# Transposing loads for the last three blocks of h and its gradients, in place of a plain load and TensorE transposes

## The chip, the cores and the metric

The kernel runs on one core of one Trainium2 chip. The metric is device time in microseconds (us) of one execution. Three runs of the kernel before gave 505.66, 508.24 and 508.82 us; the median is 508.24 us.

## The reference: what is computed

x, k, v and the incoming gradient `go` have 2048 rows and 512 columns, in bf16. The forward part is a sum of three things: x itself, a gated long convolution, and a gated feed-forward block on the normalised rows xn.

```python
xn = layernorm(x)
g, u = xn @ w_gate, xn @ w_up          # 2048 x 1376
h = g * u
out = x + conv_part(xn, k, v, shift_k, ssm_k, ssm_D) + h @ w_down
```

The program returns `out` and the gradients of all nine inputs. For the change, three of these matter: the gradients of w_down (`out_9`, 1376 x 512, h transposed times go) and of w_gate and w_up (`out_7` and `out_8`, 512 x 1376, xn transposed times the gradients of g and u). All three contract over the 2048 rows.

## The kernel before, in words

**Stages.** The first 300 us compute, for eight chunks of 256 rows each, the feed-forward block and its backward part, beside the spectral transforms of the convolution. For each chunk, `ffn1` makes three products of 1376 columns by 256 rows: h and the two gradients. They are called slots t = 0 (h), 1 and 2 (the gradients). TensorE makes them with the 1376 columns on the partitions, in 11 blocks of 128 columns (the last has 96). The first seven chunks (`NCH - 1`) are stored to the DRAM scratch tensor `HDD[P, NFB, NCH - 1, 3, 256]`, which is indexed by partition, block, chunk, slot and row; the last chunk stays in SBUF in `hds[1]`.

**The last stage**, from about 320 us on, is where the change lies. The generator `dw` walks over the 11 blocks `fb`. The weight gradients contract over the rows, so each block needs h and its gradients turned, with the 128 rows of a tile on the partitions. For that, a block is loaded back from `HDD` with one plain load of 1344 KB (`load_hb`, L799), two or three blocks ahead, into one of two buffers of the tag `hb`. `hid_t(fb, t)` (L804 to L816) then turns one slot: 16 TensorE transposes of 128 x 128 into a PSUM tile `pt` (L815; 14 from `hb`, 2 from `hds[1]`), and one ScalarE copy of 128 x 2048 from PSUM into `nath` (slot 0) or `natd` (slots 1 and 2). That copy goes through the helper `act` at L221.

In each block, in program order: 16 matmuls `pd` (L922) give the w_down gradient of the block from `nath`; the copy `od` and its store (L925); `hid_t(fb + 1, 0)` and `hid_t(fb + 1, 1)`; 32 matmuls `pu` (L939) from `natd` for columns c = 0 and 1; `hid_t(fb + 1, 2)` and `load_hb(fb + 3)`; 32 more `pu` matmuls; the copy `og`; after every second block two stores (L952). `natd` has two buffers and `nath` has one.

**Beside it** run generators that `dw` advances step by step (L1063): `inv_y` and `inv_dk` (inverse transforms on TensorE: `po` at L892, loads `gk` at L877, stores of `o5t` at L895), `dsk_gram`, and `ew`, which is the VectorE tail: `final(b)` and `bwd(b)` for eight pairs of rows. `final` loads `bb` one step ahead (L1000) and stores `o` (L1013) and `e` (L1028), each from a single buffer; `bwd` stores `dk` (L994). Near the end, `put_dD` copies a column on VectorE (L903) and transposes it on TensorE (`ptd`, L906).

**Order.** In this stage every DMA is issued from SyncE's queue (SP), in order. A planner fixes the order on each engine ahead of the run: it simulates the engines by its own costs, and among the instructions that are ready it takes the one that the program names first. An instruction whose buffer isn't free yet is ordered behind the ones that free it.

**Transposing loads already there.** `load_xt` (L475) fetches xn and go of chunks 1 to 7 with `dma_start_transpose`, 128 rows by 1024 columns (256 KB) each, 12 in all, between 31 and 241 us.

Of the kernel before, what the change touches and what calls it, by code (L numbers as in the profile page):

```python
# [8 lines left out]
BF = mybir.dt.bfloat16  # L9
# [11 lines left out]
R = 16  # L21
P = 128
NC4 = 4
FBLK = [(i * 128, min(128, F - i * 128)) for i in range((F + 127) // 128)]
NFB = len(FBLK)
NCH = 8
# [150 lines left out]
def kernel(  # L177
# [24 lines left out]
    nc = tc.nc  # L202
# [14 lines left out]
    def cs(c):  # L217
        return slice(c * 128, (c + 1) * 128)

    def act(o, i):  # L220
        nc.scalar.copy(o, i)  # L221
# [10 lines left out]
    HDD = dram.tile([P, NFB, NCH - 1, 3, 256], BF, name="HDD")  # L232
# [5 lines left out]
    def P2(name, shape, dt=F32):  # L238
        return ps2.tile(shape, dt, name=name, tag="p2")

    def P1(name, shape, dt=F32):
        return ps1.tile(shape, dt, name=name, tag="p1")

    ident = const.tile([P, P], BF, name="ident")
# [27 lines left out]
    hds = [p.tile([P, NFB, 3, 256], BF, name=f"hd{i}") for i, p in enumerate((hdp, hdl))]  # L272
# [497 lines left out]
    for tag in mainit:  # L770
        if tag == "wa":
            wa_es.close()
            c1 = ctx.enter_context(tc.tile_pool(name="c1", bufs=1, reuse_waits="tile"))
            xnC = c1.tile([P, R, D], BF, name="xnC")
            goC = c1.tile([P, R, D], BF, name="goC")
# [11 lines left out]
    c1n = ctx.enter_context(tc.tile_pool(name="c1n", bufs=1, reuse_waits="tile"))  # L787
    c1b = ctx.enter_context(tc.tile_pool(name="c1b", bufs=2, reuse_waits="tile"))
    nats = {}
# [6 lines left out]
    def load_hb(fb):  # L796
        f0, fw = FBLK[fb]
        t = c1b.tile([P, NCH - 1, 3, 256], BF, name="hb")
        nc.sync.dma_start(t[:fw], HDD[:fw, fb])  # L799
        hbs[fb] = t  # L800

    hbs = {}

    def hid_t(fb, t):  # L804
        f0, fw = FBLK[fb]
        hb = hbs.pop(fb) if t == 2 else hbs[fb]
        if t == 0:
            nats[fb, 0] = c1n.tile([P, R, P], BF, name="nath")
        elif t == 1:
            nats[fb, 1] = c1n.tile([P, 2, R, P], BF, name="natd", bufs=2)  # L810
        dst = nats[fb, 0] if t == 0 else nats[fb, 1][:, t - 1]
        pt = P2("pt", [P, R, P], BF)
        for r in range(R):
            hs = hb[:fw, r // 2, t] if r < R - 2 else hds[1][:fw, fb, t]
            nc.tensor.transpose(pt[:, r, :fw], hs[:, (r % 2) * 128:(r % 2) * 128 + 128], ident[:fw, :fw])  # L815
        act(dst[:, :, :fw], pt[:, :, :fw])  # L816

    load_hb(0)
    pend = [load_g1(0, 0), load_g1(1, 0)]
# [91 lines left out]
    def dw():  # L911
        og = None
        for t in range(3):
            hid_t(0, t)
            yield
        load_hb(2)
        for fb, (f0, fw) in enumerate(FBLK):
            last = fb + 1 == NFB
            nt = nats.pop((fb, 0))
            pd = P1("pd", [P, D])  # L920
            for r in range(R):
                nc.tensor.matmul(pd[:fw, :], lhsT=nt[:, r, :fw], rhs=goC[:, r, :], start=(r == 0), stop=(r == R - 1))  # L922
            od = c2b.tile([P, D], BF, name="od")
            act(od[:fw], pd[:fw])
            nc.sync.dma_start(out_9[f0:f0 + fw, :], od[:fw])  # L925
            yield
            if not last:
                hid_t(fb + 1, 0)
                yield
                hid_t(fb + 1, 1)  # L930
                yield
            ng = nats.pop((fb, 1))
            pu = P2("pu", [P, NC4, 2, P])
            if fb % 2 == 0:
                og = c2.tile([P, 2, NC4, 2 * P], BF, name="og")
            q0 = (fb % 2) * P
            for c in range(NC4):
                for r in range(R):
                    nc.tensor.matmul(pu[:, c, :, :fw], lhsT=xnC[:, r, cs(c)], rhs=ng[:, :, r, :fw],  # L939
                                     start=(r == 0), stop=(r == R - 1))  # L940
                if c == 1:
                    yield
                    if not last:
                        hid_t(fb + 1, 2)
                        if fb + 3 < NFB:
                            load_hb(fb + 3)
                        yield
            act(og[:, :, :, q0:q0 + fw].rearrange("p t c f -> p c t f"), pu[:, :, :, :fw])
            if fb % 2 == 1 or last:
                a = f0 - q0  # L950
                for t, o in enumerate((out_7, out_8)):
                    nc.sync.dma_start(o[:, a:f0 + fw].rearrange("(c p) f -> p c f", p=128), og[:, t, :, :q0 + fw])  # L952
            yield
# [110 lines left out]
    for n, _ in enumerate(dw()):  # L1064
        for sd in sides:
            if n >= sd[0]:
                sd[0] += sd[1]
                next(sd[2], None)
# [33 lines left out]
```

## Time and profile before

| quantity | value |
|---|---|
| median of three runs | 508.24 us |
| the profiled execution: its time / its span | 507.66 us / 505.9 us |
| TensorE busy over the span | 479.2 us (95%) |
| VectorE, ScalarE busy | 341.0 us (67%), 328.7 us (65%) |
| mean DMA rate | 278 GB/s |
| L815 transposes on TensorE | 528, first at 324.8 us, last at 488.0 us |
| L799 plain loads of `hb` | 11, at 315.7 to 461.0 us, 6.9 to 11.9 us to landing |

The span runs from the first to the last instruction; the execution's own time is 1.76 us more. A matmul's row gives its duration through the pipeline (218 ns for a transpose), although the next one starts earlier: 16 transposes in a row take 0.9 us. A row of SP gives how long the issue of a DMA held SP, not how long the data took; the time to landing counts from the start of the issue.

### The profile page before, as it was taken

To read this page: it belongs to the slowest core of one execution; us is meant where nothing else is said; L and a number is where in the kernel's file an instruction comes from. 1 tells how busy PE (TensorE), PEld (TensorE's weight loads), DVE (VectorE), ACT (ScalarE), POOL (GpSimd) and SP (SyncE) were. 2 spreads that over 40 slices of the span, in tenths; PEclk is the share of its full clock that TensorE was granted. 3 is DMA by queue.
4 is the path that set the end of the run, shared out by engine and by line. 5 is a ranking of instruction groups with operands and counts; after the bars stand their busy time and mean duration, and the time that the engine had idled before them with its cause. 6 is when DMAs were issued, how large, how long until landed. Compare 5 with 4: busy or idle time off the path is not lost.

```text
span 505.9 us, 10724 instructions
## 1 busy us (share of the span) xinstructions
PE 479.2 (95%) x4420; PEld 323.4 (64%) x4457; DVE 341.0 (67%) x633; ACT 328.7 (65%) x358; POOL 6.7 (1%) x17
## 2 busy tenths in 40 slices
PE   8789889998999999999999999999999989999996
PEld 7677554645747547547457733566776768777885
DVE  3987998888365748866648956031288987999800
ACT  3676788857837949759569975286575524555551
POOL 3000000000000000000000000020000000000000
PEclk9998999999999999999999999999999999999999
DMA  9999997989896957967968396999999999897513
GB/s 279 375 330 335 292 298 250 341 269 344 299 296 212 278 187 242 289 206 233 271 198 264 127 343 222 374 359 370 375 334 342 371 294 351 269 309 240 166 60 108
DMA packets 98045, 140.41 MB, mean 278 GB/s; under 512 B 18474, under 2 KB 72047, under 8 KB 96108
## 3 DMA queue, kind: packets, MB, share of 16 engines
q1 hardware_dynamic: 96668, 138.94, 83.3%
q10 hardware_dynamic: 1328, 0.79, 0.5%
q8 instruction: 35, 0.57, 0.5%
q14 instruction: 14, 0.11, 0.1%
HBM read 72.76 MB, written 63.41 MB: 269 GB/s over the span
## 4 chain that ended last, share of the span: by engine, by line
PE 55%; DMA 20%; DVE 10%; ACT 9%; issue 3%; SPq 2%; ACTq 0%
PE px L534 12%; PE pgu L493 9%; PE pu L939 8%; PE py L527 6%; PE pdh L499 5%; PE pd L922 4%; DMA FD<-fst 3%; PE pg L590 2%; PE pt L815 2%; PE ps L561 2%; ACT gu L221 2%; DMA out_dram<-o 2%; DMA khC<-in_A_k_dram 2%; DMA bb<-BX 2%; ACT fst L221 2%
## 5 line engine op out<-in xcount | busy, mean ns | idle before, releaser
L939 PE MATMUL pu<-natd,xnC 128*128 128x256 bf16 (+1 forms) x704 | 79.1, 270 | 0.7 <-ACT nath L221 0.7
L534 PE MATMUL px<-WT,hd 128*128 128x512 bf16 (+1 forms) x346 | 78.9, 379 | 0.5 <-issue 0.3
L939 PEld LDWEIGHTS <-xnC 128*128 128x128 bf16 x704 | 67.2, 98 | 8.7 <-issue 1.0
L534 PEld LDWEIGHTS <-hd 128*128 128x128 bf16 (+1 forms) x352 | 33.5, 98 | 42.7 <-issue 3.7
L221 ACT COPY natd<-pt 128x2048 bf16<-128x2048 bf16 (+1 forms) x22 | 40.4, 1838 | 25.4 <-PE pt L815 25.4
L493 PE MATMUL pgu<-xt,Wu 128*128 128x256 bf16 (+1 forms) x352 | 53.3, 274 | 3.5 <-DVE WdT L224 2.0
L493 PE MATMUL pgu<-xt,Wg 128*128 128x256 bf16 (+1 forms) x352 | 52.8, 273 | 0.0
L221 ACT CAST gu<-pgu 128x1024 bf16<-128x1024 f32 (+1 forms) x48 | 45.3, 946 | 11.3 <-PE pgu L493 11.0
L221 ACT CAST GO<-pg 128x1024 bf16<-128x1024 f32 x48 | 46.3, 1019 | 7.7 <-issue 4.8
L577 DVE TENSOR_TENSOR T<-SP 128x2048 bf16<-128x2048 bf16 x24 | 29.3, 1223 | 31.9 <-ACT SP L221 31.9
L499 PE MATMUL pdh<-gt,WdT 128*128 128x256 bf16 (+1 forms) x352 | 47.1, 275 | 1.5 <-DVE WdT L224 1.3
L221 ACT CAST SP<-ps 128x1024 bf16<-128x1024 f32 x48 | 46.6, 1034 | 1.9 <-PE ps L561 1.9
L221 ACT CAST fst<-pf 128x1024 bf16<-128x1024 f32 x40 | 39.2, 1034 | 12.5 <-DMA FD<-fst 10.8
L493 PEld LDWEIGHTS <-Wu 128*128 128x128 bf16 (+1 forms) x352 | 33.0, 100 | 19.9 <-issue 15.1
L527 PE MATMUL py<-Wd,hd 128*128 128x512 bf16 (+1 forms) x166 | 40.5, 380 | 0.8 <-issue 0.5
L499 PEld LDWEIGHTS <-WdT 128*128 128x128 bf16 (+1 forms) x352 | 34.9, 101 | 6.8 <-DVE WdT L224 1.5
L922 PE MATMUL pd<-goC,nath 128*128 128x512 bf16 (+1 forms) x166 | 38.3, 379 | 0.5
L221 ACT CAST bx<-px 128x512 bf16<-128x512 f32 x16 | 9.5, 592 | 45.1 <-PE px L534 45.1
L493 PEld LDWEIGHTS <-Wg 128*128 128x128 bf16 (+1 forms) x352 | 34.9, 100 | 3.6
L511 DVE TENSOR_TENSOR hd<-gu 128x512 bf16<-128x512 bf16 (+1 forms) x48 | 19.1, 398 | 24.3 <-ACT gu L221 24.2
L512 DVE TENSOR_TENSOR hd<-gu,dh 128x1024 bf16<-128x1024 bf16 (+1 forms) x48 | 30.7, 642 | 1.1 <-ACT dh L221 0.2
L527 PEld LDWEIGHTS <-hd 128*128 128x128 bf16 (+1 forms) x176 | 16.3, 98 | 22.8 <-issue 4.8
(155 smaller groups left out, 677.7 us busy)
## 6 DMA issues: line engine op xcount, KB each, us to landing
HDD<-hd SPq DMA_DIRECT2D x35, 384.0 KB, 4.8
hb<-HDD SPq DMA_DIRECT2D x10, 1344.0 KB, 11.4
FD<-fst SPq DMA_DIRECT2D x24, 512.0 KB, 3.9
X<-FD SPq DMA_DIRECT2D x24, 512.0 KB, 5.5
GD<-GO SPq DMA_DIRECT2D x24, 512.0 KB, 3.8
g<-GD SPq DMA_DIRECT2D x8, 1024.0 KB, 8.8
BX<-bx SPq DMA_DIRECT2D x8, 512.0 KB, 3.4
bb<-BX SPq DMA_DIRECT2D x8, 512.0 KB, 7.6
```

The lines of the kernel that those rows point to most:

```text
L221: nc.scalar.copy(o, i)
L493: nc.tensor.matmul(pgu[:w, i, t, :], lhsT=W[:, c, f0:f0 + w], rhs=xt[:, :, c, :], start=(c == 0), stop=(c == NC4 - 1))
L499: nc.tensor.matmul(pdh[:w, i, :], lhsT=WdT[:, c, f0:f0 + w], rhs=gt[:, :, c, :], start=(c == 0), stop=(c == NC4 - 1))
L511: nc.vector.tensor_tensor(hd[:fw, fb0:fb0 + n, 0, :], gu[:fw, :n, 0, :], gu[:fw, :n, 1, :], op=ALU.mult)
L512: nc.vector.tensor_tensor(hd[:fw, fb0:fb0 + n, 1:3, :], gu[:fw, :n], dh[:fw, :n].unsqueeze(2).to_broadcast((fw, n, 2, 256)), op=ALU.mult)
L527: nc.tensor.matmul(py[:], lhsT=hd[:fw, fb, 0, ss], rhs=Wd[:fw, fb, :], start=(fb == 0), stop=(fb == NFB - 1))
L534: nc.tensor.matmul(px[:], lhsT=hd[:fw, fb, t, ss], rhs=W[:fw, fb, :], start=(t == 1 and fb == 0), stop=(t == 2 and fb == NFB - 1))
L561: nc.tensor.matmul(ps[32 * q:32 * q + 32, a, :], lhsT=TB.EF[64 * a:64 * a + 64, 4 * g + q, ri].rearrange("p k j -> p (k j)"), rhs=X[64 * a ...
L577: tt(W[:].rearrange("p c a d -> p c (a d)"), A[:, i:i + 1].rearrange("p c a d -> p c (a d)").to_broadcast((P, 2, 2 * D)), B[:].rearrange(" ...
L590: nc.tensor.matmul(pg[q // 2][64 * a:64 * a + 64, q % 2, :], lhsT=TB.EI[32 * q:32 * q + 32, 2 * g + a, yi].rearrange("p k c -> p (k c)"), ...
L922: nc.tensor.matmul(pd[:fw, :], lhsT=nt[:, r, :fw], rhs=goC[:, r, :], start=(r == 0), stop=(r == R - 1))
L939: nc.tensor.matmul(pu[:, c, :, :fw], lhsT=xnC[:, r, cs(c)], rhs=ng[:, :, r, :fw], start=(r == 0), stop=(r == R - 1))
```

## The change

The last three blocks (8, 9, 10) no longer have a plain load or 48 TensorE transposes each. `load_nat` fetches h (d = 0) and the two gradients (d = 1) of such a block from `HDD` by transposing loads on SP, one for each of the seven stored chunks: 128 partitions by 256 columns for h, by 512 columns for the gradients. The eighth chunk is turned as before from SBUF, by six transposes in one PSUM tile (`last_t`), with two smaller copies. For h, the new tile takes a buffer of the tag `hb`; the gradients take the two buffers of `natd`.

The loads of h of block fb + 3 stand where its `load_hb` stood, in the middle of block fb; those of the gradients of block fb + 2 stand at the end of block fb. The tiles are laid out by chunk in all 11 blocks, so the copies of `hid_t` and the operands of `pd` and `pu` are indexed differently throughout.

```diff
+    def load_nat(fb, d):
+        if d:
+            nats[fb, 1] = t = c1n.tile([P, NCH, 2, 2, P], BF, name="natd", bufs=2)
+        else:
+            nats[fb, 0] = t = c1b.tile([P, NCH, 1, 2, P], BF, name="nathT", tag="hb")
+        for ch in range(NCH - 1):
+            nc.sync.dma_start_transpose(out=t[:, ch].rearrange("s t h f -> s (t h) f"),
+                                        in_=HDD[:, fb, ch, d:1 + 2 * d].rearrange("p t s -> p (t s)"))
+
+    def last_t(fb):
+        f0, fw = FBLK[fb]
+        pt = P2("pt7", [P, 3, 2, P], BF)
+        for t in range(3):
+            for h in range(2):
+                nc.tensor.transpose(pt[:, t, h, :fw], hds[1][:fw, fb, t, h * 128:h * 128 + 128], ident[:fw, :fw])
+        act(nats[fb, 0][:, NCH - 1, 0, :, :fw], pt[:, 0, :, :fw])
+        act(nats[fb, 1][:, NCH - 1, :, :, :fw], pt[:, 1:3, :, :fw])
+
+    TURNED = range(NFB - 3, NFB)
+
     def hid_t(fb, t):
+        if fb in TURNED:
+            if t == 0:
+                last_t(fb)
+            return
...
-            nats[fb, 0] = c1n.tile([P, R, P], BF, name="nath")
+            nats[fb, 0] = c1n.tile([P, NCH, 1, 2, P], BF, name="nath")
         elif t == 1:
-            nats[fb, 1] = c1n.tile([P, 2, R, P], BF, name="natd", bufs=2)
+            nats[fb, 1] = c1n.tile([P, NCH, 2, 2, P], BF, name="natd", bufs=2)
...
-        act(dst[:, :, :fw], pt[:, :, :fw])
+        act(dst[:, :, :, :fw], pt[:].rearrange("s (c h) f -> s c h f", h=2)[:, :, :, :fw])
...
-                nc.tensor.matmul(pd[:fw, :], lhsT=nt[:, r, :fw], rhs=goC[:, r, :], start=(r == 0), stop=(r == R - 1))
+                nc.tensor.matmul(pd[:fw, :], lhsT=nt[:, r // 2, 0, r % 2, :fw], rhs=goC[:, r, :], start=(r == 0), stop=(r == R - 1))
...
-                    nc.tensor.matmul(pu[:, c, :, :fw], lhsT=xnC[:, r, cs(c)], rhs=ng[:, :, r, :fw],
+                    nc.tensor.matmul(pu[:, c, :, :fw], lhsT=xnC[:, r, cs(c)], rhs=ng[:, r // 2, :, r % 2, :fw],
...
                         hid_t(fb + 1, 2)
-                        if fb + 3 < NFB:
+                        if fb + 3 in TURNED:
+                            load_nat(fb + 3, 0)
+                        elif fb + 3 < NFB:
                             load_hb(fb + 3)
...
+            if fb + 2 in TURNED:
+                load_nat(fb + 2, 1)
             act(og[:, :, :, q0:q0 + fw].rearrange("p t c f -> p c t f"), pu[:, :, :, :fw])
```

More of the change, by code (lines that the diff above doesn't have):

```diff
@@ L807, in hid_t @@
         if t == 0:
-            nats[fb, 0] = c1n.tile([P, R, P], BF, name="nath")
+            nats[fb, 0] = c1n.tile([P, NCH, 1, 2, P], BF, name="nath")
         elif t == 1:
-            nats[fb, 1] = c1n.tile([P, 2, R, P], BF, name="natd", bufs=2)
-        dst = nats[fb, 0] if t == 0 else nats[fb, 1][:, t - 1]
+            nats[fb, 1] = c1n.tile([P, NCH, 2, 2, P], BF, name="natd", bufs=2)
+        dst = nats[fb, 0][:, :, 0] if t == 0 else nats[fb, 1][:, :, t - 1]
         pt = P2("pt", [P, R, P], BF)
```

## The prediction

> **What bounds the kernel now.** I read the slices of the page first: TensorE is at nine tenths or more almost everywhere, so the question is where it is last in line. The change touches only the stage from 428 us on, so I went to the chain that ended last, in order of time (start, us, what):
>
> ```profile
> 467.25 0.91 PE pt L815 x16
> 468.16 0.02 issue
> 468.18 0.02 ACTq L221
> 468.20 0.04 issue
> 468.24 1.87 ACT nath L221
> 470.11 0.04 issue
> 470.15 3.65 PE pu L939 x32
> 473.81 0.89 PE pt L815 x16
> 474.70 3.49 PE pu L939 x32
> ...
> 496.17 5.29 PE pu L939 x64
> ```
>
> From 409 us to 501.5 us the chain never leaves TensorE, except for the copy at 468.24 and its two like. During that copy TensorE turns the next slot and does a `po`; its own idle time there is 0.22 us. So here the transposes stand on the path that sets the end, and each us of them that goes is a us gained, as long as what replaces them is in time.
>
> What replaces them is issued by SP. The rows of L475 (duration min/median/max in ns is how long SP was held):
>
> ```profile
> L475 SPq DMA_TRANSPOSE xt<-XN x5: 1276/1292/3196, 71.3 to 237.4; - x5
> L475 SPq DMA_TRANSPOSE gt<-in_grad_out_dram x5: 1322/1588/3988, 72.6 to 240.9; - x5
> L475 SPq DMA_TRANSPOSE gt<-go_b x1: 1364/1364/1364, 31.2 to 31.2; - x1
> L475 SPq DMA_TRANSPOSE xt<-xn_b x1: 3220/3220/3220, 48.2 to 48.2; - x1
> DMA to landing us min/median/max: 3.8/4.6/8.2
> ```
>
> No transposing load here held SP for less than 1.28 us. SP's timeline shows what a plain issue costs, and the places that the new loads take:
>
> ```profile
> 445.61 0.34 SPq L1028 DMA_DIRECT2D out_dram<-e  x1
> 446.92 0.28 SPq L979 DMA_DIRECT2D out_dram<-dskt  x1
> 447.30 0.34 SPq L799 DMA_DIRECT2D hb<-HDD  x1
> ...
> 458.62 0.59 SPq L877 DMA_DIRECT2D gk<-GD  x1
> ...
> 461.01 0.38 SPq L799 DMA_DIRECT2D hb<-HDD  x1
> ```
>
> A plain load of 1344 KB holds SP for 0.34 to 0.38 us, and there is room between the issues.
>
> **The change, part by part.**
>
> *TensorE, removed.* A full slot is 16 transposes in 0.89 us, 56 ns each; in block 10 (96 columns) 0.68 us, 42 ns each. Each block goes from 48 to 6, so 42 go: 42 x 56 ns = 2.35 us in blocks 8 and 9, 42 x 42 ns = 1.8 us in block 10; together 6.5 us. The two waits of 0.22 us on the copy ahead of `pu`, those of 454.87 and 470.15, go as well: 0.4 us. **Gain on the path: 6.9 us.** If all else is in time, `pu` of block 10 ends at 501.5 - 6.9 = 494.6 us.
>
> *ScalarE.* Nine copies (six of 1.86 us, three of 1.44 us) go; six small ones come. By 0.58 us for 512 elements and 1.01 us for 1024 (`od`, `og`) these are some 0.4 and 0.6 us. ScalarE was idle about half the time here, so this counts as nothing beyond the 0.4 us.
>
> *Layout in all blocks.* The 24 remaining copies now write pieces. The row nearest to that is `o5t`, which writes with a stride and takes 1.02 us for 1024 elements beside 0.99 us of `og`; I take nothing, at most 0.03 us per 1024 elements, hidden by ScalarE's idle time. `pu` reads two runs of 128 elements per matmul both before and after, only closer together; no row prices the distance, and I take nothing.
>
> *DMA data.* Three plain loads (1344 + 1344 + 1008 KB) go, 21 x 64 KB + 21 x 128 KB = 4032 KB come. The bytes hardly change. In the windows of 10 us the DMA engines' share here is 0.96, 0.64, 1.00, 0.44, 0.25 from 440 to 490 us, so there is room behind 470 us.
>
> *SP, added.* Three issues of 0.38 us become 42 transposing ones: 7 + 7 per block. No row has a transposing load of 64 or 128 KB. From below, it can't hold SP for less than a plain issue, 0.28 us; from above, the longest one measured held it 3.99 us, and the mean of the 12 is 1.94 us. How does the hold go with size? Plain issues hardly depend on it: 0.33 us for `od` of 128 KB, 0.46 us for `khC` of 2048 KB. And the quiet transposing issues lie close together, 1.28 to 1.36 us, like a fixed cost. So I stay by the nearest row, 1.28 us for the same kind of instruction, and take off little for the smaller size: **1.25 us**, an estimate.
>
> By the Trainium skill, Advanced Engine Details and Errata, section DMA Advanced Topics, transposing DMAs on this chip are as fast as regular ones. For landing this trace agrees (4.6 us median beside 3.3 to 6.9 us for plain loads of 256 KB), for the hold on SP it doesn't (1.28 us beside 0.3 to 0.6 us); if it held for both, the second rival below would be the outcome. The same skill, VectorE: DVE Perf Modes, section The three transpose paths, gives 1309 ns for one 128 x 128 by DMA and 390 ns by TensorE and prefers TensorE; paid for each tile one after the other, 3 x 42 tiles would be 165 us by that page. The trace speaks against that: eight such tiles landed 3.8 us after the issue began.
>
> *What SP must get through.* `nathT` of block 8 is issued from 428.3 us, where its `hb` load was, and costs nothing: SP has time until 444 us. From 444.1 us, when the last transposes of block 7 free the `hb` buffer, there are always loads waiting: h of 9 at once, gradients of 8 when `pu` of block 6 ends (447.7 us), gradients of 9 about 460 us, h of 10 about 464 us (it takes the buffer of h of block 8, so it waits for `pd` of block 8), gradients of 10 about 472 us. That is 35 transposing issues. Between them, 18 other DMAs that the timeline shows between 445.6 and 482.6 us (`e`, `dk`, `o`, `od`, `o5t`, `og`, one `gk`, `dskt`); counted without the time in which a full queue held them they are 7.2 us. Between issues lies about 0.08 us, 53 times: 4.2 us. With a hold of 1.25 us: 43.8 + 7.2 + 4.2 = 55.2 us, so the last issue ends at 499.3 us and began at 498.0. It lands 3.8 us later (the shortest landing, since it is smaller): 501.8 us. `pu` of block 10 needs that piece in its first of four groups; behind it are 50 of 64 matmuls, 50/64 x 5.29 = 4.1 us. End of `pu`: 506.0 us, beside 501.5 us before: **+4.5 us**. The gain on TensorE is spent waiting in front of `pu` of block 9 (its loads end about 486 us, it would like to start at 477 us) and of block 10.
>
> In general the shift is 34 us for each us of hold: nothing changes at 1.12 us, and the full 6.9 us is gained at 0.92 us and below.
>
> *Others behind SP.* A run of seven issues holds SP for about 9 us. The stores of `o` and `e` wait behind it, and VectorE writes these single buffers again about 12 us later, landing of 4 to 6 us included. So VectorE's tail (its end was at 479.3 us) slips by some us at each run. The column for `ptd` is its last work, and TensorE reached `ptd` at 482.9 us; so some of the wait may show there instead. `gk` has 20 us between its issue and its use, enough.
>
> **Rivals.**
>
> 1. *SP is the bound with a hold of 1.12 to 1.4 us* (my forecast): 507.66 + 4.5 = 512.2 us, between 507.7 and 517.2 us. For it: the quiet rows at 1.28 us. Against: nothing so small was measured.
> 2. *The hold falls with size, to 0.92 us or less; SP keeps up*: 507.66 - 6.9 = 500.8 us. For it: 1.28 us was paid for eight tiles, here there are two or four. Against: plain issues don't fall with size.
> 3. *The hold is that of a busy queue*, slower. Place: the same 35 issues. Three of the 12 held SP for 3.2 us or more, where 512 KB transfers stood ahead of them in full DMA engines. The other nine average 1.43 us, all 12 average 1.94 us: 507.66 + 34 x (1.43 - 1.12) = 518.2 us up to 507.66 + 34 x 0.82 = 535.5 us. It decides once the mean hold is over 1.4 us. For it: the new loads read pieces of 512 and 1024 bytes where L475 reads 2 KB, and stores of `o`, `e`, `dk` and `og` mix in. Against: with SP the bottleneck the DMA engines have less to do (64 KB per 1.25 us is 52 GB/s).
> 4. *It doesn't do what it says*: the planner, which has its own costs, puts the loads so late or SP's stores so early that block 8 already starves. Then time like rival 3.
>
> **How the numbers follow.** Forecast 1 has a chance of 0.50, rival 2 has 0.25, rival 3 has 0.20, rival 4 has 0.05. The predicted time is that of forecast 1, 512 us; it is made against the profiled execution (507.66 us), which is 0.6 us below the median of the runs. The range of 500 to 522 us takes in rivals 1 and 2 and the lower end of 3. Within 1% of 508.24 us (503.2 to 513.3 us, about what a measurement can tell from no change) lies a good half of forecast 1 and little of rival 2: 0.34. Slower by more: the rest of forecast 1, rivals 3 and 4: 0.40. Faster by more: 0.26.
>
> **What would show it.** In the profile after: 384 transposes at L815 and 18 of `last_t`, 24 big copies in place of 33; TensorE busy less by 6 to 7 us. The rows of the transposing issues decide: a median hold of 1.2 to 1.3 us with SP issuing without a pause from 444 to about 498 us, and TensorE waiting for `natd` ahead of the last `pu` groups, bears out forecast 1. Holds under 0.9 us and no wait of `pu` on a DMA mean rival 2. I am wrong altogether if TensorE waits somewhere that hangs on neither SP nor these loads.

## The result, and the profile after

The changed kernel takes 524.53 us (median of 5 runs, 522.09 to 525.51) where the kernel before takes 507.75 us (median of 5 runs on the same chip, 505.53 to 508.82). The ratio is 1.0336, with a 95% interval of 1.0309 to 1.0364: 3.4% slower. The forecast was 512 us with a range of 500 to 522 us; the result lies above the range. The profiled execution took 523.57 us, with a span of 521.5 us.

The page of the kernel after: the busy time of each engine, the TensorE clock in 40 slices (tenths of full speed, 13 us each), and the chain that ended last, by engine.

```profile
PE 481.4 (92%) x4331; PEld 318.5 (61%) x4331; DVE 341.2 (65%) x633; ACT 315.7 (61%) x355; POOL 6.8 (1%) x17
...
PEclk9999999999999999999999999999999999997698
...
PE 55%; DMA 14%; DVE 10%; SPq 10%; ACT 8%; issue 3%; ACTq 0%; DVEq 0%
```

ScalarE lost the copies that were taken out (328.7 to 315.7 us). TensorE has fewer instructions and yet more busy time (479.2 to 481.4 us), because its clock drops in the last slices. And SP's queue, 2% of the chain before and absent from it behind 409 us, now makes 10%. Here is the end of that chain of the kernel after, in order of time (start, us, what):

```profile
452.51 1.02 SPq L811
453.54 0.05 issue
453.59 1.24 SPq L811
...
508.53 2.90 DMA natd<-HDD
511.43 0.04 issue
511.47 5.67 PE pu L964 x52
```

From 452 us the chain goes from one transposing issue of L811 to the next, up to the last one; between 468.5 and 477.4 us it passes through a store of `dk`, VectorE and a few plain issues. In SP's own timeline no gap from 452.25 us to the end of the last issue at 509.8 us is over 0.12 us. The last data land at 511.43 us, and the last matmuls of the kernel follow. That SP would set the end was the forecast. The rows of these issues (min/median/max in ns of the time that SP was held; the last line is that of `natd`):

```profile
L811 SPq DMA_TRANSPOSE nathT<-HDD x21: 1182/1244/1957, 427.6 to 497.8; - x21
L811 SPq DMA_TRANSPOSE natd<-HDD x21: 1211/1264/2845, 461.4 to 508.5; - x21
...
DMA to landing us min/median/max: 2.4/2.8/6.6
```

The medians, 1.244 and 1.264 us, are the 1.25 us of the estimate. So the hold was right, and something else is 11 us off. SP's timeline of the kernel after shows where it begins:

```profile
427.64 8.40 SPq L811 DMA_TRANSPOSE nathT<-HDD  x6
436.14 0.52 SPq L1057 DMA_DIRECT2D out_dram<-e  x1
...
450.55 0.35 SPq L1042 DMA_DIRECT2D out_dram<-o  x1
451.15 0.33 SPq L1057 DMA_DIRECT2D out_dram<-e  x1
451.86 0.29 SPq L1008 DMA_DIRECT2D out_dram<-dskt  x1
452.25 9.02 SPq L811 DMA_TRANSPOSE nathT<-HDD  x7
```

The store of `e` at 436.14 us stands behind six transposing issues that began at 427.64 us. And the second run of issues begins at 452.25 us, where the prediction had 444.1 us: it stands behind stores of `o`, `e` and `dskt`, whose data VectorE had not made. Why VectorE was late is in two lines of its timeline (in brackets its idle time before the instruction, and what ended it):

```profile
440.54 0.69 DVE L1044 TENSOR_TENSOR e<-goC,yC 128x1024 bf16<-128x1024 bf16 x1 [6.39 <-DMA out_dram<-e]
...
471.24 0.69 DVE L1019 TENSOR_TENSOR dk<-dks,skb 128x1024 bf16<-128x1024 bf16 x1 [7.66 <-DMA out_dram<-dk]
```

VectorE may not write `e` again until the store of the old `e` has landed. That store had been held by SP's transposing issues. So SP and VectorE hold each other: SP's run delays a store, the store delays VectorE, VectorE delays the next stores, and SP, in order, delays the next run. VectorE waits 19.7 us in this way (6.39, 0.85, 7.66 and 4.82 us). TensorE's own waits are of two kinds. Two of its lines:

```profile
472.62 0.58 PE L964 MATMUL pu<-natd,xnC 128*128 128x256 bf16 x2 [2.14 <-DMA natd<-HDD]
...
490.88 0.27 PE L931 MATMUL ptd<-ident,dDs 128*4 128x128 bf16 x1 [6.42 <-DVE dDs L928]
```

For `natd` it waits 5.85 us in six pieces in `pu` of block 8 (466 to 473 us) and 3.14 us in five pieces in `pu` of block 10 (507 to 511 us). Once, for 6.42 us, it waits ahead of `ptd` for VectorE's late tail.

The windows of the kernel after (us, then the busy time of TensorE, its weight loads, VectorE, ScalarE and GpSimd in the window, the granted TensorE clock, the DMA share and GB/s):

```profile
465.00:470.00 5.00, 1.56 (x11) 0.81 (x10) 0.00 (x0) 1.18 (x2) 0.00 (x0) 0.96 0.53 125
470.00:475.00 5.00, 2.59 (x12) 1.47 (x11) 3.66 (x6) 0.00 (x0) 0.00 (x0) 0.50 0.76 233
...
485.00:490.00 5.00, 0.00 (x0) 0.00 (x0) 4.89 (x9) 0.00 (x0) 0.00 (x0) 0.67 0.57 115
490.00:495.00 5.00, 3.77 (x26) 3.00 (x27) 4.73 (x9) 2.75 (x5) 0.00 (x0) 0.50 0.50 127
```

Where TensorE did little or nothing, the granted clock is 0.50 in the window behind it; in the last matmuls, from 510 to 515 us, it is 0.66. Before, it is 1.00 in every window from 465 to 505 us.

### The profile page after: what moved, and what is told of

Its sections match the earlier page's. It is cut to its first block, busy times and chain, and to the rows that moved or that the text cites. A ratio compares the mean times of both kernels' runs of the same rounds, so it can differ in the third digit from the quotient of the medians.

```text
span 521.5 us, 10552 instructions
## 1 busy us (share of the span) xinstructions
PE 481.4 (92%) x4331; PEld 318.5 (61%) x4331; DVE 341.2 (65%) x633; ACT 315.7 (61%) x355; POOL 6.8 (1%) x17
## 4 chain that ended last, share of the span: by engine, by line
PE 55%; DMA 14%; DVE 10%; SPq 10%; ACT 8%; issue 3%; ACTq 0%; DVEq 0%
PE px L534 14%; PE pgu L493 9%; SPq L811 8%; PE py L527 7%; PE pu L964 5%; PE pdh L499 4%; PE pd L947 3%; PE pf L347 3%; PE pg L590 2%; PE pt L840 2%; PE ps L561 2%; DMA out_dram<-o 2%; ACT gu L221 2%; DMA X<-FD 2%; DMA FD<-fst 2%
## 5 line engine op out<-in xcount | busy, mean ns | idle before, releaser
L964 PE MATMUL pu<-natd,xnC 128*128 128x256 bf16 (+1 forms) x704 | 85.3, 280 | 9.6 <-DMA natd<-HDD 9.0
L964 PEld LDWEIGHTS <-xnC 128*128 128x128 bf16 x704 | 70.2, 101 | 21.4 <-issue 11.9
L221 ACT CAST og<-pu 128x1024 bf16<-128x1024 f32 (+1 forms) x11 | 10.9, 993 | 58.7 <-PE pu L964 32.0
L221 ACT COPY natd<-pt 128x2048 bf16<-128x2048 bf16 (+2 forms) x19 | 31.8, 1674 | 17.7 <-PE pt L840 17.7
L527 PE MATMUL py<-Wd,hd 128*128 128x512 bf16 (+1 forms) x176 | 41.9, 380 | 0.0
```

What stands on the lines that cost most here:

```text
L527: nc.tensor.matmul(py[:], lhsT=hd[:fw, fb, 0, ss], rhs=Wd[:fw, fb, :], start=(fb == 0), stop=(fb == NFB - 1))
```

## The experiments

Three theories are told apart. **Count**: each transposing issue holds SP for about 1.25 us whatever it moves, and SP has too many of them. **Coupling**: the time is lost because runs of issues and VectorE's stores hold each other in SP's order. **Size or layout**: the new tile layout, the pieces that are read, or the number of DMAs as such. In all of them the reckoning starts from 500.8 us, the time if the 6.9 us of TensorE are gained and nothing is late.

### Layout and the number of DMAs

The new layout in all blocks and nothing else (on the kernel after):

```diff
-    TURNED = range(NFB - 3, NFB)
+    TURNED = range(NFB, NFB)
```

> No block is turned by loads; only the layout by chunk of the copies and matmul operands stays. Theory (the loss is SP's, 42 transposing issues of 1.25 us each, in order with the other DMAs): as before the change, 507.7 us within 1.5 us. Rival (the layout makes the copies or pu slower in all 11 blocks): some us of the 16.8 us loss stay here, 510 us or more.

Measured 506.94 us, ratio 0.9982 (0.9969 to 0.9996). The layout costs nothing.

The same 42 pieces as plain loads, TensorE still turning them (on the kernel before):

```diff
-        nc.sync.dma_start(t[:fw], HDD[:fw, fb])
+        if fb >= NFB - 3:
+            for ch in range(NCH - 1):
+                nc.sync.dma_start(t[:fw, ch, 0:1], HDD[:fw, fb, ch, 0:1])
+                nc.sync.dma_start(t[:fw, ch, 1:3], HDD[:fw, fb, ch, 1:3])
+        else:
+            nc.sync.dma_start(t[:fw], HDD[:fw, fb])
```

> The kernel before, with the plain load of each of the last three blocks cut into 14, one per chunk for h and one for the gradients, as the changed kernel cuts its transposing loads. Theory (the hold of the transposing kind is what costs): plain issues hold SP for 0.35 to 0.5 us, SP keeps up: 505 to 511 us. Rival (any run of seven or fourteen DMAs in SP's order costs it): 513 us or more.

Measured 506.42 us, ratio 0.9979 (0.9960 to 0.9999). The row of the issues of the two gradients:

```profile
L802 SPq DMA_DIRECT2D hb<-HDD x21: 304/430/1102, 430.2 to 474.2; - x21
```

A plain load of the same piece holds SP for 0.43 us (median), a third of a transposing one, and 42 of those fit. Their data land 2.6 us after the issue began (median), those of the transposing pieces 2.8 us. So it is neither the number of DMAs nor the size of the pieces; it is that they transpose.

### What sets the hold: the number of issues, not the bytes

Each transposing load cut in two, 84 issues for the same bytes (on the kernel after):

```diff
-            nc.sync.dma_start_transpose(out=t[:, ch].rearrange("s t h f -> s (t h) f"),
-                                        in_=HDD[:, fb, ch, d:1 + 2 * d].rearrange("p t s -> p (t s)"))
+            to = t[:, ch].rearrange("s t h f -> s (t h) f")
+            ti = HDD[:, fb, ch, d:1 + 2 * d].rearrange("p t s -> p (t s)")
+            for i in range(2):
+                n = 1 + d
+                nc.sync.dma_start_transpose(out=to[:, i * n:(i + 1) * n], in_=ti[:, i * n * 128:(i + 1) * n * 128])
```

> The changed kernel with each transposing load cut in two (128 x 128 and 128 x 256): 84 issues, the same bytes. Theory (a fixed hold per issue): holds stay at 1.2 to 1.25 us, 42 x 1.25 us more on a bound SP: 570 us, between 555 and 585. Rival (the hold follows the bytes): holds of 0.6 us, 522 to 530 us.

Measured 578.65 us in a single run (span 576.8 us). The row of the pieces of h:

```profile
L815 SPq DMA_TRANSPOSE nathT<-HDD x42: 1109/1230/2243, 427.4 to 542.7; - x42
```

128 x 128 (32 KB) holds SP for 1.230 us by this row, where the whole piece took 1.244 us; the halves of the gradients, 128 x 256, hold it for 1.244 us, the whole ones for 1.264. Half the bytes, the same hold. The 42 additional issues lengthen the span by 576.8 - 521.5 = 55.3 us, 1.32 us each: the median hold of 1.24 us, and 0.08 us for the gaps (0.04 to 0.05 us) and for a few longer holds. With that many issues the count alone accounts for the added time.

The other way: one load of 128 x 768 for each chunk, h and gradients together, 21 issues. The eighth chunk gets a small tile of its own.

```diff
+        t = hbs[fb] = c1b.tile([P, NCH - 1, 3, 2, P], BF, name="natT", tag="hb")
         for ch in range(NCH - 1):
-            nc.sync.dma_start_transpose(out=t[:, ch].rearrange("s t h f -> s (t h) f"),
-                                        in_=HDD[:, fb, ch, d:1 + 2 * d].rearrange("p t s -> p (t s)"))
+            nc.sync.dma_start_transpose(out=t[:, ch].rearrange("s t h f -> s (t h) f"),
+                                        in_=HDD[:, fb, ch].rearrange("p t s -> p (t s)"))
...
+        t8 = c1n.tile([P, 3, 2, P], BF, name="nat8", tag="natd", bufs=2)
+        act(t8[:, :, :, :fw], pt[:, :, :, :fw])
...
```

> Same bytes, one transposing load per chunk for all three slots (128 x 768), 21 issues in place of 42. Theory (a fixed hold of 1.25 to 1.3 us per issue): holds stay at 1.25 to 1.3 us, SP gets through in time, TensorE's gain of 6.9 us comes out almost whole: 500.8 to 504 us. Rival (the hold follows the bytes or the DMA engines' pace for transposing): holds of 1.8 us and more, 517 to 525 us.

Measured 512.96 us, ratio 1.0100 (1.0067 to 1.0132). Better than after, but 9 us above what was expected of it. The hold is the expected one, 1.285 us (median). What is late is one run, by the SP timeline of this kernel:

```profile
483.09 4.69 SPq L1029 DMA_DIRECT2D out_dram<-dk  x2
487.87 9.26 SPq L809 DMA_TRANSPOSE natT<-HDD  x7
```

SP has issued nothing since 479.6 us: it waits for VectorE's `dk`, and begins block 10's loads at 487.87 us. VectorE itself had waited 8.3 us in all for stores behind earlier runs. The queue had room, but not at the place in its order where the loads of block 10 stand.

And one load for a whole block, 128 x 5376 (1344 KB), 3 issues (on the kernel with one load per chunk):

```diff
-        for ch in range(NCH - 1):
-            nc.sync.dma_start_transpose(out=t[:, ch].rearrange("s t h f -> s (t h) f"),
-                                        in_=HDD[:, fb, ch].rearrange("p t s -> p (t s)"))
+        nc.sync.dma_start_transpose(out=t[:].rearrange("s c t h f -> s (c t h) f"),
+                                    in_=HDD[:, fb].rearrange("p c t s -> p (c t s)"))
```

> Same bytes, one transposing load per block (128 x 5376), 3 issues in place of 42. Theory: SP is held a few us per block at most, the gain on TensorE comes out: 500.8 us within 2 us. Rival (the hold follows the bytes): some 18 us per issue, 517 to 525 us.

Measured **500.22 us, ratio 0.9842 (0.9819 to 0.9865)**: faster than both kernels, and the 500.8 us of the reckoning to within 0.6 us. (Beside the kernel before in the same series, 507.52 us, the gain is 7.3 us.) The row of the three loads:

```profile
L808 SPq DMA_TRANSPOSE natT<-HDD x3: 5533/6596/6761, 427.7 to 475.1; - x3
...
DMA to landing us min/median/max: 8.6/8.6/8.6
```

The three loads hold SP for 18.9 us in all; the 42 hold it for more than 52. VectorE waits 0.7 us for stores. TensorE has no idle time from 440 to 493 us. The instructions of TensorE are the same 4331 as after, so the two can be subtracted. From 440 us to the end of the span: 58.0 us with TensorE busy for 53.6 us here, 81.5 us with TensorE busy for about 61.4 us after. Of 23.5 us, 7.8 us are the same matmuls at a lower clock, and 15.7 us are waiting. That is TensorE's account; not all of it lies on the path that sets the end.

The same for the last five blocks (`range(NFB - 5, NFB)`):

> One transposing load per block as in e3_per_block, for the last five blocks in place of three. Theory: two more blocks give 42 x 56 ns + 0.22 us = 2.6 us each on TensorE's path, if the loads come in time: 495 us within 2 us. Rival (before 428 us the DMA engines are full, so the longer hold and the slower transposing stand in the way of loads that VectorE and TensorE wait for): no better than 500 us.

Measured 499.35 us, ratio 0.9843 (0.9805 to 0.9881): no further gain that can be told.
The five loads hold SP for 11.06, 9.08, 5.32, 8.77 and 6.44 us, and the DMA engines' share during these holds is 1.16, 1.20, 1.01, 1.15 and 1.03. So the hold of a large load isn't fixed, and the longer ones fall where the share is higher; no run varies that alone. Two of the three long ones are those of the added blocks, at 399 and 421 us. TensorE waits 2.52 us for one of the loads ahead of `pd`.

The 42 issues on ScalarE's queue:

```diff
-            nc.sync.dma_start_transpose(out=t[:, ch].rearrange("s t h f -> s (t h) f"),
+            nc.scalar.dma_start_transpose(out=t[:, ch].rearrange("s t h f -> s (t h) f"),
```

> The changed kernel with the 42 transposing loads issued from ScalarE's queue in place of SP's. Theory (the hold is the issuing sequencer's): ScalarE is held 1.2 to 1.3 us per issue, 52 us on top of some 35 us of its own from 428 us on, and TensorE waits for its copies behind runs of seven: 515 to 530 us. Rival (the hold is a trait of SP or of its full queue): 508 us or less.

Measured 536.53 us, ratio 1.0573 (1.0554 to 1.0593). A line of TensorE's timeline:

```profile
470.02 1.87 PE L917 MATMUL po<-IW,gk 128*128 128x128 bf16 x16 [14.53 <-ACT og L221]
```

The median hold is 1.27 us on ScalarE's queue too (1.266 and 1.287): it goes with the queue that issues, on both queues that were tried. ScalarE's copies stand behind a run of issues, and TensorE waits 14.53 us for one of them. The theory had the direction right, but the time is 6.5 us above the top of its range.

### Where the 8 us at the start of the second run came from

A second buffer for `o` and `e` for the late pairs, so that VectorE need not wait for the store of the old one (on the kernel after):

```diff
-        o = c2.tile([P, 2, D], BF, name="o0")
+        o = c2b.tile([P, 2, D], BF, name="o0b", tag="vb") if b >= 4 else c2.tile([P, 2, D], BF, name="o0")
-        e = c2.tile([P, 2, D], BF, name="e")
+        e = c2b.tile([P, 2, D], BF, name="eb", tag="kb") if b >= 4 else c2.tile([P, 2, D], BF, name="e")
```

> The changed kernel, with a second buffer for o and e from the fifth pair of rows on, so that VectorE need not wait for a store that stands behind a run of loads. Theory of the coupling (a run of loads delays a store, the store delays VectorE, and SP then waits in order for VectorE ahead of the next run): VectorE's waits of 6.4 and 4.8 us for e go, the second run starts near 445 us in place of 452 us, 516 to 519 us. Rival (the number of issues alone): no change, 522 to 526 us.

Measured 525.29 us, ratio 1.0358 (1.0322 to 1.0395): no gain; the expectation failed. VectorE's timeline:

```profile
444.31 0.69 DVE L1041 TENSOR_TENSOR o0b<-o0b,bb 128x1024 bf16<-128x1024 bf16 x1 [4.90 <-DMA bb<-BX]
```

The wait for the store of `e` is gone, and the load of `bb`, which stands behind the same first run, is late in its place. The second run began at 452.66 us. A run of seven holds up everything behind it; taking away one of the waits shows the next.

No transposing loads for h of block 8, so no first run; 35 issues are left (a plain load and TensorE transposes of slot 0 instead):

```diff
+        if fb == FIRST and not d:
+            load_hb(fb)
+            return
...
+    FIRST = NFB - 3
...
-            return
+            if t or fb != FIRST:
+                return
...
```

> The changed kernel, but h of block 8 comes by the plain load and 16 TensorE transposes as before; its gradients and all of blocks 9 and 10 stay with transposing loads. So the run of seven issues at 428 us is gone, and the 35 issues of the prediction's sum remain. Theory (that run delays a store, VectorE and so the start of the next run by 8 us): the next run starts at 444 to 447 us, the time is 513 to 518 us. Rival (the late start has another cause, and only the number of issues in the long stretch counts): 522 us or more.

Measured 523.18 us, ratio 1.0326 (1.0299 to 1.0353). The theory's first half holds and its second fails. SP's timeline:

```profile
446.36 9.97 SPq L813 DMA_TRANSPOSE nathT<-HDD  x7
...
495.76 2.88 SPq L1028 DMA_DIRECT2D out_dram<-dk  x2
498.73 9.09 SPq L813 DMA_TRANSPOSE natd<-HDD  x7
```

Without the first run the next one begins at 446.36 us, six us earlier than after. So the first run was what moved it. But those six us are lost again: VectorE now waits for stores behind the later runs (4.66, 5.56 and 9.11 us), SP needs 61.5 us from there to the end of the last issue instead of 57.5, and TensorE waits 13.66 us ahead of `ptd` for VectorE's tail. For the last loads it doesn't wait at all: `pu` of block 10 runs through. What released `pu` of block 9 is another engine's copy:

```profile
498.57 8.85 PE L969 MATMUL pu<-natd,xnC 128*128 128x256 bf16 x64 [3.95 <-ACT og L221]
```

The chain that ended last goes back from there to this copy, to a store of `og` that SP issued at 492.67 us behind a run of seven, and into that run. ScalarE may not write `og` again until that store has landed (497.4 us). So a run reaches TensorE on a second way, through a store of ScalarE's.

Fewer blocks: the last two, 28 issues (`range(NFB - 2, NFB)`), and the last one, 14 issues (`range(NFB - 1, NFB)`).

> Only blocks 9 and 10 by transposing loads, 28 issues. By the count alone SP has time for them (about 50 us of 52 from 444 us on) and TensorE gains 2.4 + 0.2 + 1.8 = 4.4 us: 503 to 506 us. By the theory that each run of seven also shifts the stores, VectorE and what SP waits for in order: 508 to 514 us.

> Only block 10 by transposing loads, 14 issues, from 460 us on. By the count SP has time, TensorE gains 1.8 us: 505 to 506 us. With the shift through stores and VectorE, whose column for ptd TensorE waits for at 483 us: 507 to 510 us.

Measured 518.24 us (1.0193, 1.0147 to 1.0239) and 508.53 us (1.0018, 0.9997 to 1.0038). Both are slower than the count alone would make them; the first is slower than the coupling theory gave as well. There, too, no `pu` waits for a load: TensorE waits 7.08 us ahead of `ptd` for VectorE, then 4.95 us for the copy `og`, whose old store stands behind a run. With one block, TensorE was to gain 2.0 us, and 2.8 us are lost against that.

All stores of `o`, `e` and `dk` on GpSimd's queue instead of SP (`nc.gpsimd` for `nc.sync` at L1023, L1042 and L1057):

> The changed kernel, with the stores of o, e and dk issued from POOL's queue in place of SP's (26 transfers less in SP's order). Theory (SP's order couples the loads to VectorE's stores: a late store holds the loads behind it, and a late load run holds the stores): the long run of loads starts near 444 us in place of 452 us, and VectorE no longer waits for e and dk: 508 to 513 us. Rival (only the number of issues counts): nine stores fewer in the stretch, 9 x 0.5 = 4.5 us, 520 us.

Measured 538.21 us (1.0607, 1.0571 to 1.0644), where a gain was expected. This run decides nothing between the theories: the stage ahead changed too, and the first run of issues began at 444.88 us instead of 427.64 us.

So only the late stores, of pairs that fall in this stage, were moved (on the kernel after):

```diff
-        nc.sync.dma_start(o2_n[:, rb, :], dk[:])
+        (nc.gpsimd if b >= 3 else nc.sync).dma_start(o2_n[:, rb, :], dk[:])
-        nc.sync.dma_start(o0_n[:, rb, :], o[:])
+        (nc.gpsimd if b >= 5 else nc.sync).dma_start(o0_n[:, rb, :], o[:])
-        nc.sync.dma_start(o1_n[:, rb, :], e[:])
+        (nc.gpsimd if b >= 4 else nc.sync).dma_start(o1_n[:, rb, :], e[:])
```

The store of `dskt` went with them.

> The changed kernel, with only the late stores that depend on VectorE (o from pair 5, e from pair 4, dk from pair 3, and dskt) issued from POOL's queue; 42 transposing issues stay on SP, and the stage up to 427 us is as in the changed kernel. Theory of the coupling (SP waits in order for VectorE, VectorE waits for stores behind runs, TensorE waits for VectorE's column at ptd): these waits go, SP runs from 444 to about 498 us, 508 to 512 us. Rival (35 holds of 1.3 us are enough by themselves to explain the loss): 518 us or more.

Measured 519.53 us, ratio 1.0239 (1.0180 to 1.0299). SP's timeline:

```profile
446.14 11.82 SPq L811 DMA_TRANSPOSE nathT<-HDD  x7
458.07 10.28 SPq L811 DMA_TRANSPOSE natd<-HDD  x7
...
496.55 9.04 SPq L811 DMA_TRANSPOSE natd<-HDD  x7
```

None of VectorE's late stores is in this queue now. It starts at 446.14 us and issues without a pause until 505.6 us, VectorE is done at 484.5 us, and TensorE doesn't wait ahead of `ptd`. Still the kernel takes 519.5 us: 35 issues in 51.2 us, 1.46 us each with the gaps, and eight us of other DMAs between them set when the last loads land, for which `pu` of block 10 waits 2.5 us. (ScalarE's stores of `og` still stand behind a run, and TensorE waits 8.01 us for that copy ahead of `pu` of block 9; but SP never pauses.) The coupling theory had 508 to 512 us here; it falls as the sole cause.

The same stores moved with 21 issues (on the kernel with one load per chunk):

> As e2_per_chunk (21 issues, one per chunk), with the late stores of o, e, dk and dskt issued from POOL's queue. Theory of the coupling: the load of block 10 no longer stands behind stores that wait for VectorE, SP has time for 21 issues, TensorE's gain comes out: 500 to 503 us. Rival (VectorE's stores are not what held e2_per_chunk back): 510 us or more.

Measured 511.46 us (1.0073, 1.0043 to 1.0104), not the 500 to 503 us that were expected. Block 10's loads now begin at 473.85 us, in time, but TensorE waits 7.65 us ahead of `ptd` for VectorE.

And the control, the same stores moved in the kernel before, where no run of issues stands:

> The kernel before, with the same late stores on POOL's queue, as a control for the two others. SP isn't the bound there, nor VectorE at the end: 507.5 us within 2 us by every theory.

Measured 516.38 us, ratio 1.0179 (1.0152 to 1.0206): this move by itself costs 8.5 us. VectorE waits for these stores four times, 10.5 us in all, and TensorE 6.52 us ahead of `ptd`.

So the two kernels above with moved stores aren't clean: they pay a price of their own, and how much of their time is that isn't known. What the control does show is that VectorE's tail with `ptd` behind it is a second path that is nearly critical in the kernel before: VectorE's column is ready at 479.3 us there, and TensorE comes to `ptd` at 482.9 us.

The numbers side by side. "All in time" is the profiled time of before, 507.7 us, less what TensorE gains with that many blocks:

| kernel | transposing issues | all in time, us | measured, us | lost, us | VectorE's waits for stores, us |
|---|---|---|---|---|---|
| one load per block | 3 | 500.8 | 500.2 | -0.6 | 0.7 |
| last block only | 14 | 505.7 | 508.5 | 2.8 | 4.9 |
| one load per chunk | 21 | 500.8 | 513.0 | 12.2 | 8.3 |
| last two blocks | 28 | 503.3 | 518.2 | 14.9 | 10.4 |
| without the first run | 35 | 501.6 | 523.2 | 21.6 | 19.7 |
| after | 42 | 500.8 | 524.5 | 23.7 | 19.7 |

The loss rises with the number of issues, and VectorE's waits rise with it. With 84 issues (from 461 us on), and with 42 when none of VectorE's late stores is in the queue, SP issues without a pause and the last matmuls wait for its last loads: there the count is enough. With 14 to 28 issues SP has pauses, in which it stands in order behind stores that VectorE hasn't made (with the last two blocks, from 459.8 to 464.3 us), and with the last two blocks, as without the first run, TensorE waits for `ptd` and `og` and not for the last loads. So the coupling is seen as well, through VectorE and through ScalarE. How the loss splits between the count and the coupling **stays open**, since moving the stores has a price of its own and no run takes away `og`'s.

## Why the prediction was wrong

**The bound and the hold were right; what the runs do to other engines' stores stood in the sum at nothing.** SP became the bound, with a hold of 1.24 to 1.26 us (median), and the last matmuls waited for `natd` of block 10. Rival 3 had this time, 518 to 536 us, but not for its reason: it asked for a mean hold above 1.4 us, and the 35 issues took 1.37 us each with a gap of 0.04 to 0.05 us, so their mean hold is about 1.33 us. Rival 2, a hold that falls with size, is refuted by the halves. Rival 4's sign is there: block 8 starves, its `pu` waits 5.85 us for `natd`. The first run was issued where the prediction had it (427.64 us), and the second is late behind VectorE's stores; whether another order by the planner would have spared this, no run shows.

**The sum, term by term.** `pu` of block 10 was to end at 506.0 us and ended at 517.1 us:

| term | predicted | measured | difference, us |
|---|---|---|---|
| the run of 35 begins | 444.1 | 452.25 | +8.15 |
| from there to the last issue | 53.9 | 56.3 | +2.4 |
| its landing | 3.8 | 2.9 | -0.9 |
| the matmuls behind it | 4.1 | 5.67 | +1.6 |

1. **The step that failed** is that the stores behind a run enter the sum with their issue time alone, first in *"`nathT` of block 8 ... costs nothing: SP has time until 444 us"*. SP had the time; VectorE, which needs SP's other DMAs in those 8 us, hadn't. The prediction even says, under "Others behind SP", that stores of `o` and `e` wait behind a run and that VectorE's tail slips, but it gave that no price, let it end in a wait at `ptd` and didn't carry it back to SP, where VectorE's stores stand ahead of the next run. The runs showed a start 8.15 us late, and VectorE's column for `ptd` ready at 490.8 us, where it was ready at 479.3 us before. It isn't the first run alone: without it the start is early and the time is 523.18 us all the same, since the later runs do the same to VectorE and to ScalarE's `og`. And had the loads of block 10 come in time, that alone would have brought the end of `pu` forward by the 3.14 us that it waits for them and at most 1.4 us of clock, to some 512.6 us (an estimate), still 6.6 us behind the forecast.
2. *The start at 444.1 us* was too early even without that. The lines that the prediction itself shows have the `hb` load of before at 447.30 us, behind `dskt` at 446.92 us. In SP's order the load stands behind a store that isn't ready, however free the load's buffer is. The undisturbed start is 446.1 to 446.4 us (the kernel without the first run, the one with the late stores moved, the one with a load per block). Of the 8.15 us, some 2.2 are this, and 5.9 the slip through VectorE.
3. *Holds and others, 55.2 us:* a little small, 57.5 us. The median hold was met; a few of 1.7 to 2.8 us raise the mean with its gaps to 1.37 us.
4. *Landing 3.8 us:* 2.9 us. The smaller load does land sooner.
5. *4.1 us of matmuls behind it:* 52 matmuls need the last piece and not 50 (52/64 x 5.29 = 4.3 us), and this was taken at full clock; the granted clock was 0.66 there. By the Trainium skill, TensorE: Matmul & The Clock Gate, Part 1, an idle window of about 3.4 us puts the clock to a half, and about 3.4 us of work bring it back. At the wait ahead of `ptd` this trace agrees: 0.00 us of work from 485 to 490 us and 0.50 behind it. At two other places less was enough: from 465 to 470 us TensorE worked 1.56 us in pieces, and the clock fell when no wait had been over 1.35 us; from 507 to 511 us it fell when none had been over 0.90 us. The prediction counted TensorE's waits at their own length only. By the comparison with the load per block, the lower clock adds 7.8 us of TensorE time; most of it lies ahead of waits for SP, and in this sum it is 5.67 - 4.3 = 1.4 us.

**What was right.** The gain of 6.9 us on TensorE's path comes out when nothing is late (500.22 us against 500.8). The layout costs nothing. The hold hardly depends on the size up to 128 x 768 (1.23 to 1.29 us). That the queue pays by the issue is seen in the 55.3 us for 42 more issues.

**The two pages that were weighed.** That transposing DMAs are as fast as regular ones (the Trainium skill, Advanced Engine Details and Errata, DMA Advanced Topics) holds here for the landing, 2.8 us beside 2.6 us, and not for the issue: 1.24 us beside 0.43 us for the same piece. The 1309 ns for one 128 x 128 (VectorE: DVE Perf Modes, The three transpose paths) is near what one issue of that size holds a queue here, 1.23 us. It isn't a price per tile: 42 tiles of one load hold it for 5.5 to 6.8 us and land in 8.6 us, about 0.2 us a tile.

**The signs that were named.** The bigger copies and the transposes went as said. TensorE's busy time was to fall by 6 to 7 us: it rose by 2.2 us after, and fell by 5.7 us with a load per block (479.2 to 473.5 us). "TensorE waits somewhere that hangs on neither SP nor these loads" didn't come: the wait ahead of `ptd` is for VectorE, and VectorE's waits end with stores that SP held.

## What to carry to other kernels

A transposing load costs its queue by the issue, about 1.25 us here whether it carries 32 or 192 KB, so make it large: three loads of 1344 KB gain 1.6% where 42 small ones lose 3.4%. Where a queue is filled in order, price a run of issues by what stands behind it and who needs that, and follow the chain until it comes back to the queue: a store that lands late holds the engine that rewrites its buffer, and that engine's next store holds the next run. A stretch of some us in which TensorE mostly waits is to be counted with the slower clock behind it, if the work behind it sets the end.

## What the runs showed of the hardware that was not expected

- The hold of a transposing issue is flat in size: 1.230 us at 128 x 128, 1.244 at 128 x 256, 1.264 at 128 x 512, 1.285 at 128 x 768 (medians), and 1.27 us on ScalarE's queue. At 128 x 5376 it isn't fixed: 5.3 to 6.8 us in five loads and 8.8 to 11.1 us in three others, where the DMA engines' share was 1.15 to 1.20 in place of 1.01 to 1.04.
- TensorE's granted clock falls to 0.50 after a stretch in which it did little, also where the work came in pieces with no wait over 0.90 us between them (507 to 511 us). 64 matmuls of `pu` behind the wait at `ptd` took 8.89 us, where 64 at full clock in the same trace (block 7) took 7.15 us.
- Stores moved from SP to GpSimd's queue made the unchanged kernel 8.5 us slower: VectorE waited four times for them, 2.0 to 3.6 us each, where it had waited once, 0.30 us.
